# One greedy pass instead of tried orders: a change to the planner that writes out a kernel's instruction order

## The chip, the cores and the metric

The kernel runs on one core of one Trainium2 chip, as one program. The metric is the device time of that program in microseconds (us). Before the change the median of three runs is 1660.0 us (1659.27 to 1660.18). In the profile the engines are called PE (TensorE, the matrix products), PEld (its weight loads), DVE (VectorE), ACT (ScalarE), POOL (GpSimd) and SP (SyncE, which issues DMA transfers).

## The reference

All numbers are float32. An attention block without softmax feeds a mixture of four experts (8 batches, 8 heads, 576 tokens, 64 values a head; 4608 tokens of 512 values; experts of width 1024):

```python
kv  = np.einsum('bhsd,bhse->bhde', k, v)
o   = np.einsum('bhsd,bhde->bhse', q, kv)
x   = o / np.sqrt(np.mean(o * o, -1, keepdims=True) + 1e-06) * g_norm   # then to (4608, 512)
p   = domain_probs / (domain_probs.sum(-1, keepdims=True) + 1e-09)
for e in range(4):
    out += p[:, e:e+1] * (np.maximum(x @ w1[e], 0.0) @ w2[e])
```

## The kernel before, in words

**Steps.** The 4608 tokens are cut into nine chunks of 512: chunk c < 8 holds the first 512 tokens of batch c, and chunk 8 the 64 tokens that each batch has left over. The main loop runs over 4 experts x 9 chunks = 36 steps, numbered s = 0 to 35. A step has an up part (x @ w1 and the ReLU, `up`, line 1256; a plain form for step 0, `up_plain`, line 1360) and a down part (h @ w2, `down` at line 1488 or `down_deep` at line 1538), and the down part of step s is spread over the up part of step s + 1. While expert 0 is at work, `attention` (line 899) prepares the chunk after the present one; `opening` (line 760) prepares batch 0. A step past the opening takes some 43 to 53 us.

**Products by sevens.** Both parts use a Strassen-like scheme that makes a 2x2 block product of seven products, nested twice. So `up` has seven multipliers in the order `OUTER = (1, 2, 6, 5, 3, 7, 4)` and, for each, seven products in the order `ORDER = (1, 6, 2, 5, 7, 4, 3)`. One such product is 4 matmul calls; float32 takes two passes each, so the profile shows it as 8 matmuls of 128x128 on line 478 (`halves_of`). In the down part one unit is 8 or 16 of these, or 16 matmuls of 128x256. The forms that the products read (sums and differences of blocks) are made by `combine` (line 501) on DVE or POOL.

**Banks and copies.** A product's result lands in a PSUM bank. There are two each of four kinds: u1 and u2 for the up part, db and ab for the down part and for attention. For each multiplier, product 1 fills the bank u1, ACT copies it into the bank u2 as a seed (line 1305), product 2 adds onto the seed, and ACT copies that out as a block of the result (line 1305, out `big`). Products 6 and 7 are copied out as snapshots (line 1305, out `snap`), which DVE adds to products 5 and 3 (line 1313). The same pattern stands in `down_deep` at lines 1623 (ACT) and 1631 (DVE). Since a bank is filled again as soon as it has been read, most products wait for one ACT copy or one DVE sum that reads an earlier product. What stands between the two on PE is set by the order alone. Attention's rows are turned by PE into an ab bank (`turn_x`, line 1069) and copied by ACT in two halves (line 1081); the turn of the left-over rows is `turn_left` (line 1091); the key-value products are `key_values` (line 999); q, k and v come by loads on SP (line 507).

**What sets the order.** The scheduler of the framework is switched off (`manual_schedule`). Every piece of work is an `Op` with a key (its place in the sequence of steps, such as 19.06), a cost per engine that may run it, and its dependences. `Plan.layout` (line 94) plays the program through with these costs before the kernel is built, and writes down in which order each engine's operations start; the order list, and nothing else of it, becomes the program. At each moment each engine takes one operation that could start: PE and SP the first by key, the others the one that is due first. An operation may be taken up to 1.1 (PE) or 0.9 (DVE, ACT, POOL) of a step ahead of the first one pending. Combinations that DVE or POOL may make go to whichever is free. `begin` (line 310) books an operation; for an SP transfer it computes when it lands. In front of the first products PE is kept busy by transposes of the identity (line 1765).

`layout` does this step by step. For each step it saves its state, plays this step and the next one eight times (`TRIES, LOOK, SPREAD = 8, 1, 1`), the first time with the due times as they are and then with random shifts of 1 us, takes the draw with the least modelled idle time of PE, restores the state and plays the step for good:

```python
for step in sorted(steps):
    begin = self.save()
    ...
    for n in range(self.TRIES):
        ...
            op.due = op.base + (draw.gauss(0.0, self.SPREAD) if n else 0.0)
        if self.run(step + 1 + self.LOOK):
            tried.append((self.t - self.worked, n))
        self.restore(begin)
    n = min(tried)[1]
```

Of the kernel before, what the change touches and what calls it, by code (L numbers as in the profile page):

```python
# [41 lines left out]
class Plan:  # L42
# [18 lines left out]
    TRIES, LOOK, SPREAD = 8, 1, 1  # L61
# [32 lines left out]
    def layout(self, slots, later, idle, idle_banks, idle_until):  # L94

        self.idle = idle, idle_banks, idle_until
        self.free = {k: [(0.0, i) for i in range(len(v))] for k, v in slots.items()}
        self.slots = {k: list(v) for k, v in slots.items()}
        self.later = list(later)
        self.all_bufs = list(dict.fromkeys(b for op in self.ops for b in op.bufs))  # L100
        self.live = {}
        for b in self.all_bufs:
            self.live[b.kind] = self.live.get(b.kind, 0) + 1
        self.ended = {}
        self.todo = {e: [] for e in self.REACH}
        for n, op in enumerate(self.ops):
            op.n = n
            for e in op.cost:
                self.todo[e].append(op)
        for e in self.todo:  # L110
            self.todo[e].sort(key=lambda o: (o.key, o.n))
        keys, begun, spent = [], [], 0.0
        for op in self.todo["PE"]:
            keys.append(op.key)
            begun.append(spent)
            spent += op.cost["PE"]
# [4 lines left out]
        for op in reversed(self.ops):  # L121
            for d in op.deps:
                cross = self.SAME if op.cost.keys() == d.cost.keys() else self.CROSS
                d.due = min(d.due, op.due - cross - min(d.cost.values()))
        for op in self.ops:
            op.base = op.due
        self.missing, self.after = {}, {op: [] for op in self.ops}
        for op in self.ops:
            self.missing[op] = len(op.deps)
            for d in op.deps:  # L130
                self.after[d].append(op)
        self.waiting = {k: {} for k in self.SHARED}
        for op in self.ops:
            if not self.missing[op]:
                self.arm(op)
        self.first, known = {k: {} for k in self.INORDER}, set()
        for op in self.ops:
            for b in op.outs:
                if b.kind in self.first and b not in known:
                    known.add(b)  # L140
                    self.first[b.kind][op] = True
        self.busy = {e: 0.0 for e in self.todo}
        self.worked = 0.0
        self.bus, self.port = 3.8, 0.0
        self.lanes = [0.0] * self.LANES
        self.t = 0.0
        self.wake = [0.0, 1.6]
        self.left = len(self.ops)
        self.order = []

        steps = {}
        for op in self.ops:
            steps.setdefault(math.floor(op.key), []).append(op)
        for step in sorted(steps):
            begin = self.save()
            tried = []
            for n in range(self.TRIES):
                draw = random.Random(100 * n + step)
                for op in steps[step] + steps.get(step + 1, []):
                    op.due = op.base + (draw.gauss(0.0, self.SPREAD) if n else 0.0)  # L160
                if self.run(step + 1 + self.LOOK):
                    tried.append((self.t - self.worked, n))
                self.restore(begin)
            n = min(tried)[1]
            draw = random.Random(100 * n + step)
            for op in steps[step] + steps.get(step + 1, []):
                op.due = op.base + (draw.gauss(0.0, self.SPREAD) if n else 0.0)
            assert self.run(step + 1)
        self.run(math.inf)
        assert not self.left  # L170
        self.length = max(o.end for o in self.order)
        return self.order

    def save(self):
        copied = {
            name: {k: type(v)(v) for k, v in getattr(self, name).items()}
            for name in ("free", "slots", "todo", "waiting", "first")
        }
        copied.update({name: dict(getattr(self, name)) for name in ("live", "ended", "missing", "busy")})
        copied.update({name: list(getattr(self, name)) for name in ("later", "lanes", "wake", "order")})  # L180
        copied.update({name: getattr(self, name) for name in ("worked", "bus", "port", "t", "left")})
        return (
            copied, [(o.start, o.end, o.eng) for o in self.ops],
            [(b.left, b.slot, b.ap) for b in self.all_bufs],
        )

    def restore(self, saved):
        copied, ops, bufs = saved
        for name, value in copied.items():
            if isinstance(value, dict):  # L190
                value = {k: type(v)(v) if isinstance(v, (dict, list)) else v for k, v in value.items()}
            elif isinstance(value, list):
                value = list(value)
            setattr(self, name, value)
        for o, (o.start, o.end, o.eng) in zip(self.ops, ops):
            pass
        for b, (b.left, b.slot, b.ap) in zip(self.all_bufs, bufs):
            pass

    def arm(self, op):  # L200
        for b in op.outs:
            if b.kind in self.waiting and b.slot is None and "SP" not in op.cost:
                self.waiting[b.kind][op] = max([d.end for d in op.deps] or [0.0])

    def claimed(self, kind, op):
        return sum(
            1 for o, since in self.waiting[kind].items()
            if o.due < op.due and since <= self.t + self.AHEAD and o is not op
        )

    def ready(self, op, eng, front):
        when = 0.0
        for d in op.deps:
            if d.start is None:
                return None
        for d in op.deps:
            when = max(when, d.end + (self.SAME if d.eng == eng else self.CROSS))
        need = {}
        for b in op.outs:
            if b.kind is not None and b.slot is None:  # L220
                need[b.kind] = need.get(b.kind, 0) + 1
        for k, n in need.items():
            free = self.free[k]
            spare = self.SPARE.get(k, 0) if k != "xf" or op.key < self.FORMS else 0
            ahead = op.key > front + 0.1 and (eng == "SP" or op.early)
            if len(free) < n + (spare if ahead else 0):
                return None
            if k in self.waiting and len(free) < n + self.claimed(k, op):
                return None
            if k in self.first and any(o.due < op.due for o in self.first[k] if o is not op):  # L230
                return None
            when = max(when, sorted(free)[n - 1][0])
        if eng == "SP":
            when = max(when, self.lanes[0])
        if op.port:
            when = max(when, self.port)
        return when

    def run(self, until):

        wake, todo, busy = self.wake, self.todo, self.busy
        idle, idle_banks, idle_until = self.idle
        while self.left:
            t, moved = self.t, False
# [3 lines left out]
            if front >= until:  # L248
                return True
            for eng in todo:  # L250
# [10 lines left out]
                for op in pending:  # L261
# [8 lines left out]
                    when = self.ready(op, eng, front)  # L270
# [12 lines left out]
                if best is not None:  # L283
                    self.begin(best, eng)
                    moved = True
                if eng == "PE" and busy[eng] <= t and 1.6 <= t and front < idle_until:
                    kind, spare = next((
                        (k, f) for k in idle_banks for f in self.free[k] if f[0] <= t
                    ), (None, None))
                    if spare is not None:  # L290
# [3 lines left out]
                        op.fn = lambda eng, bank=self.slots[kind][spare[1]]: idle(bank)  # L294
                        busy[eng] = op.end
                        self.free[kind].remove(spare)
                        self.free[kind].append((op.end, spare[1]))
                        heapq.heappush(wake, op.end)
                        self.order.append(op)
# [5 lines left out]
            if not wake:  # L305
                return False
            self.t = heapq.heappop(wake)
        return True

    def begin(self, op, eng):  # L310
        t, wake, free = self.t, self.wake, self.free
        op.start, op.eng = t, eng
        if eng == "SP":
            self.busy[eng] = t + op.cost[eng]
            self.bus = max(self.bus, t + 1.5) + op.kb / 215.0
            op.end = self.bus + 0.5
            self.lanes = self.lanes[1:] + [op.end]
# [1498 lines left out]
```

## Time and profile before

| | |
|---|---|
| median of 3 runs | 1660.0 us |
| the profiled execution itself | 1660.0 us |
| its span, first to last instruction | 1657.7 us |
| PE busy | 1648.2 us (99%) |
| DVE, ACT, POOL busy | 1230.4, 978.0, 707.7 us (74, 59, 43%) |
| granted TensorE clock | 1.000 |
| DMA: mean rate | 140 GB/s, 220 to 235 GB/s in the first 124 us |

The profile is of one core. A row of a timeline gives the start in us, the length in us, engine, line, operation, out<-in, shape and count; in brackets stands the idle time before it and who ended it. PE works in a pipeline: a matmul of 128x128 is shown as 273 ns long, but the next one starts after some 55 ns, so the length of a PE row is the distance of its starts plus a tail of about 0.17 us. A wait of PE that is shorter than this tail shows no idle time at all; it is read from the distance of starts.

### The profile page before, as it was taken

The page shows a single profiled execution, that of the slowest core. Times are in us where ns is not written, and L with a number is a line of the kernel's source. Part 1 is how long each engine was busy: PE and PEld are TensorE (multiplying, and loading weights), DVE is VectorE, ACT ScalarE, POOL GpSimd, SP SyncE. Part 2 cuts the span into 40 slices and gives each one's busy share as a digit, 9 for nine tenths or more (in the row PEclk, how much of TensorE's full clock was granted, in tenths as well). Part 3 has the DMA queues.
Part 4 walks back from the last instruction along what each step waited for, and adds up shares of the span by engine and source line. Part 5 has one row for each costly group of instructions (what it writes and reads, how often), then busy time and mean ns, then how long its engine had stood idle before and what let it go on. Part 6 is the DMA issues. An engine that isn't in the chain of part 4 may idle for free.

```text
span 1657.7 us, 66538 instructions
## 1 busy us (share of the span) xinstructions
PE 1648.2 (99%) x28990; PEld 1557.9 (94%) x28990; DVE 1230.4 (74%) x2150; ACT 978.0 (59%) x2421; POOL 707.7 (43%) x671
## 2 busy tenths in 40 slices
PE   8999999999999999999999999999999999999998
PEld 6688888888899999999999999999999999999996
DVE  4677768776877778777778787777778787777774
ACT  3465555554456665666556666666666566666662
POOL 4542232223244454553345554433455545443341
PEclk9999999999999999999999999999999999999999
DMA  9985665624475353544558444444577544444442
GB/s 221 208 235 140 195 174 157 164 100 164 146 202 139 96 136 112 133 118 120 149 150 193 115 117 122 108 110 113 141 185 176 120 124 117 117 106 114 116 104 52
DMA packets 202860, 232.44 MB, mean 140 GB/s; under 512 B 92936, under 2 KB 142536, under 8 KB 202568
## 3 DMA queue, kind: packets, MB, share of 16 engines
q1 hardware_dynamic: 179016, 191.41, 38.9%
q0 software_dynamic: 23552, 36.78, 14.4%
q8 instruction: 227, 3.72, 0.9%
q14 instruction: 65, 0.53, 0.1%
HBM read 153.95 MB, written 74.19 MB: 138 GB/s over the span
## 4 chain that ended last, share of the span: by engine, by line
PE 99%; issue 0%; ACT 0%; POOL 0%; DVE 0%; POOLq 0%
PE u L478 48%; PE db L478 32%; PE ab L478 15%; PE ab L1004 1%; PE ab L1031 1%; PE ab L1072 1%; PE ab L1765 0%; PE ab L789 0%; PE ab L809 0%; PE db L1040 0%; PE db L829 0%; PE ab L1093 0%; PE ab L844 0%; PE db L864 0%; ACT big L1453 0%
## 5 line engine op out<-in xcount | busy, mean ns | idle before, releaser
L501 DVE TENSOR_TENSOR big<-big,big 128x256 f32<-128x256 f32 (+1 forms) x568 | 517.4, 931 | 23.7 <-ACT big L1269 11.8
L478 PE MATMUL u<-xf,big 128*64 128x128 f32 x7072 | 513.3, 273 | 0.0
L478 PEld LDWEIGHTS u<-xf,big 128*64 128x64 f32 x7072 | 412.6, 137 | 5.6 <-issue 0.7
L478 PE MATMUL u<-xf,w1y 128*64 128x128 f32 x5304 | 392.4, 273 | 0.0
L478 PE MATMUL db<-big,big 128*64 128x128 f32 (+1 forms) x4208 | 352.5, 308 | 0.1
L1313 DVE TENSOR_TENSOR big<-u,snap 128x256 f32<-128x256 f32 x468 | 196.9, 422 | 202.8 <-PE u L478 154.1
L478 PEld LDWEIGHTS u<-xf,w1y 128*64 128x64 f32 x5304 | 310.4, 137 | 2.8 <-issue 0.8
L1305 ACT ACTIVATE snap<-u 128x256 f32<-128x256 f32 x490 | 187.6, 383 | 185.1 <-PE u L478 163.5
L478 PEld LDWEIGHTS db<-big,big 128*64 128x64 f32 x4208 | 257.0, 137 | 40.9 <-issue 0.8
L501 POOL TENSOR_TENSOR big<-big,big 128x256 f32<-128x256 f32 (+1 forms) x151 | 212.1, 1409 | 177.3 <-DVE big L501 94.6
L1305 ACT ACTIVATE big<-u 128x256 f32<-128x256 f32 x468 | 178.3, 383 | 68.6 <-PE u L478 43.1
L501 POOL TENSOR_TENSOR big<-big 128x512 f32<-128x512 f32 (+1 forms) x95 | 116.4, 1226 | 145.6 <-DVE big L501 88.0
L1623 ACT ACTIVATE snap<-db 128x256 f32<-128x256 f32 (+1 forms) x230 | 82.3, 358 | 137.0 <-PE db L478 123.2
L1269 ACT ACTIVATE big<-big 128x1024 f32<-128x1024 f32 x136 | 142.9, 1051 | 4.5 <-DVE big L501 3.4
L1631 DVE TENSOR_TENSOR big<-ab,snap 128x256 f32<-128x256 f32 x170 | 71.6, 421 | 69.6 <-ACT snap L1623 37.2
L1476 POOL DMA_DIRECT2D out_dram<-big x120 | 104.3, 1097 | 42.7 <-ACT big L1453 35.9
L1305 ACT ACTIVATE u<-u 128x256 f32<-128x256 f32 x245 | 90.9, 372 | 35.4 <-PE u L478 24.0
L1661 POOL TENSOR_TENSOR big<-big 128x512 f32<-128x512 f32 x27 | 34.4, 1274 | 150.7 <-DVE big L501 129.5
L478 PE MATMUL db<-w2y,big 128*64 128x128 f32 x1328 | 97.7, 273 | 0.0
L1453 ACT ACTIVATE big<-big,p_all 128x256 f32<-128x256 f32 x198 | 93.7, 500 | 1.4 <-POOL big L1661 0.7
L478 PE MATMUL db<-small,big 128*64 128x128 f32 x1248 | 93.2, 273 | 0.5 <-ACT snap L1623 0.5
L501 DVE TENSOR_TENSOR big<-big 128x512 f32<-128x512 f32 (+1 forms) x114 | 91.4, 806 | 0.5 <-PE db L478 0.4
(188 smaller groups left out, 2314.3 us busy)
## 6 DMA issues: line engine op xcount, KB each, us to landing
xf<-x SPq DMA_DIRECT2D x104, 512.0 KB, 3.8
xf<-x_h SPq DMA_DIRECT2D x85, 256.0 KB, 3.4
out_dram<-big POOLq DMA_DIRECT2D x80, 256.0 KB, 6.3
xf<-x SPq DMA_DIRECT2D x78, 256.0 KB, 3.7
x<-xf SPq DMA_DIRECT2D x36, 512.0 KB, 3.9
big<-in_moe_w_dram SPq DMA_DIRECT2D x29, 512.0 KB, 5.9
x_h<-big SPq DMA_DIRECT2D x18, 512.0 KB, 3.3
big<-in_moe_w_dram POOLq DMA_DIRECT2D x18, 512.0 KB, 7.2
```

The costliest lines, as they stand in the source:

```text
L478: nc.tensor.matmul(out_[cols], lhsT=lhsT[:, cols], rhs=rhs, **kw)
L501: lambda eng: adder(eng).tensor_tensor(out=out_(), in0=a(), in1=b(), op=op),
L1004: nc.tensor.matmul(bank.ap[r * D:(r + 1) * D, o * D:(o + 1) * D], lhsT=ks[r], rhs=vs[r], start=(j == 0), stop=(j == len(sets) - 1), skip_g ...
L1031: nc.tensor.matmul(raw[r].ap[c * D:(c + 1) * D, (o * NR + t) * D:(o * NR + t + 1) * D], lhsT=qt.ap[half, col:col + D], rhs=kv.ap[half, o * ...
L1269: lambda eng: nc.scalar.activation(out=b.ap[:], in_=b.ap[:], func=ACT.Relu),
L1305: lambda eng: nc.scalar.activation(out=where(), in_=ps.ap[:, 0:HN], func=ACT.Copy),
L1313: lambda eng: nc.vector.tensor_tensor(out=block(whole, a, t), in0=src.ap[:, 0:HN], in1=add_.ap[:], op=ALU.add),
L1453: lambda eng: nc.scalar.activation(out=cell(i, half), in_=ap(), func=ACT.Copy, scale=prob()),
L1476: nc.gpsimd.dma_start(out=dst, in_=cell(i)[parts, :], accum_op=ALU.add)
L1623: lambda eng: nc.scalar.activation(out=where(), in_=group_of(ps.ap), func=ACT.Copy),
L1631: lambda eng: nc.vector.tensor_tensor(out=cell(tq, dq), in0=group_of(src.ap), in1=group_of(add_.ap), op=ALU.add,),
L1661: lambda eng: adder(eng).tensor_tensor(out=whole(to), in0=whole(a), in1=whole(b), op=ALU.add),
```

## The change

The words that go with the change tell of batch 0 from contiguous loads with tokens at 9p+j, products pair of heads by pair, probabilities fetched early by GpSimd, and chunk 0's forms in expert 1. All these stand in both kernels. The diff touches `Plan` alone:

- The tries go, and with them `save` and `restore`. There is one pass, with the due times unshifted. `run`, `ready`, `arm`, `claimed` and `begin` are folded into `layout`.
- The model of an SP transfer differs. Before, it joins the bus 1.5 us after its issue and lands 0.5 us after its turn; after the change these are 0.6 and 1.9 us. The bus is free at first from 3.8 us before, and from 2.6 us after.
- The kernel proper, its operations, their keys, costs and dependences are the same, so that only the order on each engine and the choice between DVE and POOL (or ACT and DVE) can differ.

```diff
-    TRIES, LOOK, SPREAD = 8, 1, 1
...
-        self.bus, self.port = 3.8, 0.0
+        bus, port = 2.6, 0.0
...
-        for step in sorted(steps):
-            begin = self.save()
-            tried = []
-            for n in range(self.TRIES):
-                draw = random.Random(100 * n + step)
-                for op in steps[step] + steps.get(step + 1, []):
-                    op.due = op.base + (draw.gauss(0.0, self.SPREAD) if n else 0.0)
-                if self.run(step + 1 + self.LOOK):
-                    tried.append((self.t - self.worked, n))
-                self.restore(begin)
-            n = min(tried)[1]
-            draw = random.Random(100 * n + step)
-            for op in steps[step] + steps.get(step + 1, []):
-                op.due = op.base + (draw.gauss(0.0, self.SPREAD) if n else 0.0)
-            assert self.run(step + 1)
-        self.run(math.inf)
...
+        while left:
+            moved = False
             while todo["PE"] and todo["PE"][0].start is not None:
                 todo["PE"].pop(0)
             front = todo["PE"][0].key if todo["PE"] else 1e9
-            if front >= until:
-                return True
...
-            self.bus = max(self.bus, t + 1.5) + op.kb / 215.0
-            op.end = self.bus + 0.5
+                        bus = max(bus, t + 0.6) + op.kb / 215.0
+                        op.end = bus + 1.9
```

In the built programs the change shows as follows. Every operation of one is in the other. PE has 46 transposes of the identity in place of 44, the two more in front of the first key-value product. Past them the order on PE is the same up to 63 us, on SP up to 64 us, on ACT up to 42 us, on DVE and POOL up to 45 us of the profile before. In step 16 and in steps 32 to 36 (36 is the last down part) PE, ACT, DVE and POOL have the same order in both, and SP has it in most steps from 11 on. DVE has 4 instructions fewer, ACT 6 fewer and POOL 10 more. In step 1 SP loads the last quarter of v of batch 2 (`v2_3`, two transfers) 17 transfers later than before.

## The prediction

> **What bounds the kernel now.** I read the page's parts 1 and 4 first (does one engine set the end?), then PE's waits, the windows, and timelines at PE's few waits. From the page, and the list of PE's waits over the whole span (engine and line, for whom, us in total, times, longest):
>
> ```profile
> span 1657.7 us, 66538 instructions
> PE 1648.2 (99%) x28990; PEld 1557.9 (94%) x28990; DVE 1230.4 (74%) x2150; ACT 978.0 (59%) x2421; POOL 707.7 (43%) x671
> PE 99%; issue 0%; ACT 0%; POOL 0%; DVE 0%; POOLq 0%
> ```
>
> ```profile
> PE ab L789 <- issue: 1.6, 1, 1.6
> PE db L829 <- issue: 1.5, 1, 1.5
> PE ab L1765 <- POOL ident masks.py:199: 1.4, 1, 1.4
> PE db L478 <- ACT snap L1623: 0.5, 1, 0.5
> ```
>
> PE is the chain from start to end and hardly ever stands: 1657.7 - 1648.2 = 9.5 us, of which 1.4 lie before its first instruction, 1.5 and 1.6 are two pauses in the opening (at 13 and 19 us), 0.5 is a wait at 1627 us, and 4.4 the tail after its last matmul. In between it is full (window, length, busy us of PE, PEld, DVE, ACT, POOL, clock, DMA share, GB/s):
>
> ```profile
> 41.40:1616.00 1574.60, 1574.41 (x27968) 1504.90 (x27966) 1191.91 (x2075) 952.12 (x2361) 680.04 (x639) 1.00 0.54 140
> ```
>
> So a new order has almost nothing to win: it takes no work from PE, and outside the start and the tail there are some 4 us of waits. It can lose whatever waits it puts in.
>
> **The price of a product placed too near.** A changed order harms PE where a product follows too closely the one whose copy it needs. First the pace, undisturbed (start, length):
>
> ```profile
> 1441.25 0.61 PE L478 MATMUL ab<-small,big 128*64 128x128 f32 x8
> 1441.68 0.61 PE L478 MATMUL ab<-kv,big 128*64 128x128 f32 x8
> 1442.12 0.61 PE L478 MATMUL u<-xf,w1y 128*64 128x128 f32 x8
> ```
>
> A product starts every 0.437 us and shows 0.61. The trace of before has a few products too near. At 88 us, PE and ACT:
>
> ```profile
> 88.29 1.75 PE L478 MATMUL u<-xf,big 128*64 128x128 f32 x24
> ...
> 88.94 0.38 ACT L1305 ACTIVATE snap<-u 128x256 f32<-128x256 f32 x1
> 89.38 0.42 PEld L478 LDWEIGHTS u<-xf,big 128*64 128x64 f32 x8 [0.29 <-ACT snap L1305]
> ```
>
> The product that starts at 88.29 ends at 88.90; ACT starts its snapshot 0.04 later and takes 0.38; the product that waited for it starts at 89.38. From start to start that is 1.09 us. The waiting product stands second behind the first, where 2 x 0.437 = 0.874 was its turn: **0.22 us** lost. Directly behind, it would lose 1.09 - 0.437 = **0.65**; third behind (1.31) nothing. The second price is seen too, at the end:
>
> ```profile
> 1626.39 1.04 PE L478 MATMUL db<-w2y,big 128*64 128x128 f32 x16
> 1627.90 0.66 PE L478 MATMUL db<-small,big 128*64 128x128 f32 x8 [0.47 <-ACT snap L1623]
> ```
>
> Two products take 1.51 us to the next start in place of 0.874: the third needs the copy of the second, and 0.64 is lost.
>
> **The change, part by part.** The work on PE is the same but for two transposes. DVE has 4 instructions fewer, ACT 6 fewer, POOL 10 more; DVE is 74% busy, so a moved combination costs only where PE wants it next. So the change is worth what its order puts in as waits, less those it removes. I went through the new order and counted, for every product that needs an ACT copy or a DVE sum of an earlier product, how far behind it stands. Counted in the old order, the same way gives five waits in all: 0.34, 0.22 and 0.22 in step 1 (the last vanishes behind the second), 0.55 and 0.12 in the last down part. The trace shows 0.31 (a product at 67.97, the next at 68.71, less 0.437), 0.22, 0.64 and 0.13. The count finds every wait and is right to 0.1 us. In the new order it finds:
>
> - *Step 1, around 63 to 67 us.* Product 2 of multiplier 1 directly behind product 1: 0.65. Then `turn_left` (line 1091) directly behind the second `turn_x` (line 1069), whose first half-copy on ACT (line 1081, 0.68) must free its bank: the turn shows 1.19 and PE's next turn comes after 1.02, so 1.19 + 0.05 + 0.68 + 0.06 - 1.02 = 0.96. Then product 1 of multiplier 2 needs the second half-copy, 0.63 later, behind a `turn_left` of 0.37: 0.26. Sum 1.87.
> - *Steps 4 and 6.* Product 4 of multiplier 2 second behind product 7: 0.22, and on ACT a 0.6 us evacuation of attention starts just ahead of the snapshot and holds it 0.12 longer: 0.34 each, 0.68.
> - *Step 7.* Product 1 of multiplier 3 second behind the product whose copy frees its bank, 0.22; a down unit waits for its bank until ACT and DVE have merged the one before (0.50 + 0.48, lines 1453 and 1460, behind two snapshots), 0.35. Sum 0.57.
> - *Steps 9 to 13, 24, 27.* Four places within 0.03 to 0.14 of their turn, 0.44 if all come; I take half, 0.22.
> - *Step 19.* Product 5 of multiplier 1 directly behind product 2 of multiplier 2, whose copy frees its bank: 0.65. A product 4 second behind a product 7: 0.22. A seed of `down_deep` stands in ACT's order behind a 1.05 us negation of a weight block: 0.31. Sum 1.18.
> - *Step 28.* The same neighbours as in step 19: 0.65. Product 3 directly behind product 5, whose DVE sum (0.42, line 1313) must have read the bank, 1.13 - 0.437 = 0.70. One more second-behind: 0.22. Sum 1.57.
>
> In steps 32 to 36 the orders are equal and the end's waits stay. The other steps have none. Sum 1.87 + 0.68 + 0.57 + 0.22 + 1.18 + 1.57 = 6.1; gone with the old order of step 1: 0.31 + 0.22 = 0.5. **Net +5.6.**
>
> *The opening.* Two more transposes of the identity before the first key-value product, at the pace there (8 in 1.09 us with the tail): 0.13 each. They are hidden if the 1.49 us pause that follows covers them. Between 0 and +0.27; I take 0.1, as the pause is the nearest row.
>
> *v of batch 2.* Two transfers (`v2_3`) are moved behind 17 others on SP (16 of q, one store). Eight of q take 4.32 us to issue (65.96), so 17 come 9.2 us later. Its reader `key_values` has 2.1 us to spare now (landed at 69.36, read at 71.45) and itself moves back 6.1 us in PE's order, by the products now ahead of it: 2.1 - 9.2 + 6.1 = -1.0. The 1.87 of waits ahead of it in the same step cover that, as long as SP isn't held by them: eight of the q loads wait for the second `turn_x`, which stands behind only 0.65 of those waits. So its cost is between nothing and, at SP's slowest gaps and the longest landing of such loads there (6.8 against its own 4.7), some 1.0 + 2.1 = 3. I take 0, since its own row says 4.7. The other loads of SP and the accumulating weight load of step 19 (9.6 us on POOL's queue; such loads have a median of 7.2) move by one or two places and land with at most 0.1 to catch up; from -0.3 to +0.9.
>
> *The clock.* The pauses of 1.49 and 1.63 us stand in windows with a granted clock of 1.00; all waits above are single and shorter than 1.0. So a wait costs its own length and no more. The Trainium skill ("TensorE: Matmul & The Clock Gate", section "HAM oscillation — how this bites in real kernels") speaks against filling PE's order with waits, as pauses of over 3.4 us make the clock fall to half. By that rule only a wait for `v2_3` near its upper end, joined to the others, could come near; it would then add some 1.7 us (an estimate from that page). No row of before shows it.
>
> The profiled execution took 1660.0 us, which is also the median of the runs, 2.3 more than its span. 1660.0 + 5.6 + 0.1 = **1665.7 us**.
>
> **The rivals.**
>
> 1. *The waits stand, and `v2_3` comes late.* For: the DMA engines are over 90% busy up to 83 us, and PE's margin is negative without the other waits. Against: its own landing row. It would add 1 to 3: 1667 to 1669, with landings worse than any there 1671.
> 2. *Not slower by anything to be measured: the opening's pauses go.* One mechanism, at 13 and 19 us: PE stands 1.5 and 1.6 us for nothing that the profile names ("issue"). They come after its 222nd and its 349th matmul. If the two added transposes shift them to where PE would wait for a copy anyway, 3.1 us are given back: 5.7 - 3.1 = 2.6, 1662.6 us, inside 0.2%. It decides from 2.4 us given back on. Against: both pauses would have to go, and two matmuls are a small shift.
> 3. *The order does less than the count says.* Places where I have ACT or DVE held by other work (0.24 in steps 4 and 6, 0.35, 0.22, 0.31, 0.70: together 1.8) come out free, because these engines run ahead more than their order shows: 5.7 - 1.8 = 3.9, 1663.9. With half the 0.65s read too high as well it ends under 1663.3. For: ACT is only 59% busy. Against: the count on the old order erred by less than 0.1 a place.
>
> **How the numbers follow.** About 0.2% (3.3 us) is what a measurement of this kernel can tell from no change. Chances: the forecast with its small errors (1663.3 to 1668), 0.68; rival 1 beyond that, 0.14; rival 2, 0.08, of which 0.01 faster; rival 3 under 1663.3, 0.09; anything that makes it faster besides, 0.01. So slower 0.82, same 0.16, faster 0.02. The range goes from rival 2's 1662.3 to rival 1's upper end, 1670.5: what lies outside is some 0.06 below and 0.07 above, and a little for what I haven't thought of.
>
> **What would show it.** In the profile after, PE's waits should appear on ACT lines 1241, 1017 and DVE line 1249 (the old 1305, 1081 and 1313), at some 63 to 70, 230, 335, 395, 905 and 1290 us, none over 1.1; PE's busy time only about 2 us up, since waits under the 0.17 tail are shown as busy in part; the two pauses near 13 and 19 us; the wait of 0.5 near the end. `v2_3` should land within 0.3 us of its reader's turn. It is wrong if PE waits for a DMA over 1 us, if a long wait stands in a step that I call free (8, 14 to 18, 20 to 23), or if the clock falls below 1.00.

## The result, and the profile after

After the change the median is 1665.62 us (1665.14 to 1665.92), beside 1659.63 us (1658.87 to 1660.18) before: a ratio of 1.0036 with a 95% interval of 1.0019 to 1.0053, so 6.0 us slower. Two single executions of the experiments below fell far out of all others (4969 us of `newdma_turn`, 9892 us of `v_early_turn`) and are left out of the ratios. The profiled execution took 1665.3 us with a span of 1663.6. Lines of the code after are those of before less 64: the products are on line 414, ACT's copies on 1241 and 1559, DVE's sums on 1249 and 1567, `combine` on 437.

The page after, its parts 1 and 4:

```profile
span 1663.6 us, 66539 instructions
PE 1650.9 (99%) x28992; PEld 1558.8 (94%) x28992; DVE 1252.9 (75%) x2146; ACT 980.6 (59%) x2415; POOL 694.4 (42%) x681
PE 97%; DVE 1%; issue 1%; ACT 0%; POOL 0%; DMA 0%; SPq 0%; DVEq 0%; POOLq 0%; ACTq 0%
```

The list of PE's waits of the kernel after (for whom, us in total, times, longest):

```profile
PE ab L725 <- issue: 1.7, 1, 1.7
PE db L765 <- issue: 1.5, 1, 1.5
PE u L414 <- DVE big L1249: 0.8, 2, 0.6
PE db L414 <- ACT snap L1559: 0.7, 2, 0.5
PE u L414 <- ACT small L1241: 0.5, 1, 0.5
PE u L414 <- ACT big L1241: 0.5, 1, 0.5
PE u L414 <- ACT u L1241: 0.5, 1, 0.5
PE ab L1029 <- ACT big L1017: 0.3, 1, 0.3
```

And its windows, over the same stretch as before:

```profile
41.40:1616.00 1574.60, 1571.27 (x27862) 1499.90 (x27860) 1210.47 (x2064) 951.18 (x2347) 666.88 (x649) 1.00 0.54 140
```

The two pauses of the opening stand as they were, the clock is 1.00, and PE is still the chain. New are seven waits of 0.2 to 0.6 us for ACT's copies and DVE's sums. The idle time in this window is 3.3 us, 3.1 more than before; the other half of the loss lies under the tails of PE's rows, as told of the profile before, and is read from the distance of starts. Counted so, against each shape's undisturbed pace, PE's last product starts 5.90 us later than before, and this divides as follows:

| stretch of the span | predicted | measured | what is in it |
|---|---|---|---|
| opening, to 60 us | +0.1 | +0.09 | two transposes |
| 60 to 100 us (step 1) | +1.34 | +0.64 | 0.64, 0.41, 0.07, 0.40 new; 0.31, 0.22 gone |
| 100 to 500 us (steps 4, 6, 7) | +1.25 | +1.19 | 0.31, 0.31, 0.22 |
| 500 to 1400 us (steps 9 to 28) | +2.97 | +3.97 | 0.16, 0.13; 0.71, 0.22, 0.13; 0.08, 0.38; 0.73, 0.82, 0.22 |
| end | 0 | 0.01 | 0.64 and 0.13 in both |

The last column is the time by which single products start late. What it lacks to the measured column are many differences of 0.05 to 0.15 where PE goes from one kind of work to another, and 0.05 behind each wait (shown below). The dearest place is step 28, on PE (start, length, idle time before it and who ended it):

```profile
1291.57 0.64 PE L414 MATMUL u<-xf,w1y 128*64 128x128 f32 x8
1292.01 0.64 PE L414 MATMUL u<-xf,big 128*64 128x128 f32 x8
1293.17 0.66 PE L414 MATMUL u<-xf,w1y 128*64 128x128 f32 x8 [0.53 <-ACT big L1241]
1294.43 1.09 PE L414 MATMUL u<-xf,w1y 128*64 128x128 f32 x16 [0.60 <-DVE big L1249]
```

From 1292.01 to 1293.17 are 1.16 us in place of 0.44: a product directly behind the one whose copy it needs. From 1293.17 to 1294.43 are 1.26: directly behind one whose DVE sum must first have read the bank.

### The profile page after: what moved, and what is told of

The parts are those of the page before. It is cut to its first block, busy times and chain, and to the rows that moved or that the text cites. A ratio compares the mean times of both kernels' runs of the same rounds, so it can differ in the third digit from the quotient of the medians.

```text
span 1663.6 us, 66539 instructions
## 1 busy us (share of the span) xinstructions
PE 1650.9 (99%) x28992; PEld 1558.8 (94%) x28992; DVE 1252.9 (75%) x2146; ACT 980.6 (59%) x2415; POOL 694.4 (42%) x681
## 4 chain that ended last, share of the span: by engine, by line
PE 97%; DVE 1%; issue 1%; ACT 0%; POOL 0%; DMA 0%; SPq 0%; DVEq 0%; POOLq 0%; ACTq 0%
PE u L414 47%; PE db L414 32%; PE ab L414 14%; PE ab L967 1%; PE ab L940 1%; PE ab L1008 1%; DVE big L437 0%; PE ab L1701 0%; PE ab L725 0%; PE ab L745 0%; DVE big L1597 0%; PE db L976 0%; PE ab L1029 0%; DMA small<-in_q_dram 0%; PE db L765 0%
## 5 line engine op out<-in xcount | busy, mean ns | idle before, releaser
L437 DVE TENSOR_TENSOR big<-big,big 128x1024 f32<-128x1024 f32 (+1 forms) x592 | 549.5, 950 | 26.6 <-ACT big L1205 8.6
L414 PE MATMUL u<-xf,big 128*64 128x128 f32 x6496 | 474.5, 273 | 0.1
L414 PEld LDWEIGHTS u<-xf,big 128*64 128x64 f32 x6496 | 381.3, 137 | 4.7 <-issue 0.7
L414 PE MATMUL db<-big,big 128*64 128x128 f32 (+1 forms) x4368 | 368.3, 307 | 0.7 <-ACT snap L1559 0.7
L414 PEld LDWEIGHTS db<-big,big 128*64 128x64 f32 x4368 | 269.0, 137 | 39.9 <-issue 2.1
L437 POOL TENSOR_TENSOR big<-big,big 128x256 f32<-128x256 f32 (+1 forms) x157 | 206.0, 1316 | 196.5 <-DVE big L437 101.2
L1559 ACT ACTIVATE snap<-db 128x256 f32<-128x256 f32 (+1 forms) x230 | 82.2, 358 | 121.5 <-PE db L414 109.2
L414 PE MATMUL db<-small,big 128*64 128x128 f32 (+1 forms) x1528 | 116.7, 274 | 0.0
L437 DVE TENSOR_TENSOR big<-big 128x512 f32<-128x512 f32 (+1 forms) x121 | 102.1, 853 | 0.0
L414 PE MATMUL ab<-big,big 128*64 128x128 f32 (+1 forms) x1384 | 97.5, 276 | 0.0
L414 PEld LDWEIGHTS db<-small,big 128*64 128x64 f32 x1528 | 90.8, 137 | 0.9 <-issue 0.2
```

What stands on the lines that cost most here:

```text
L414: nc.tensor.matmul(out_[cols], lhsT=lhsT[:, cols], rhs=rhs, **kw)
L437: lambda eng: adder(eng).tensor_tensor(out=out_(), in0=a(), in1=b(), op=op),
L1559: lambda eng: nc.scalar.activation(out=where(), in_=group_of(ps.ap), func=ACT.Copy),
```

## The experiments

**Theories.** A: the one pass places products too near the copies that they need, and the tries of before were what took these places out; each costs its distance. B: the changed landing model of SP's transfers does it, since other loads come late. C: the old order is a tuned whole, and any other order costs some time. For step 1, D came up on the way: DVE works in order and stands at a transposition of q whose load has not landed, with a sum behind it that PE needs.

### One half of the change at a time

`tries_newdma` is the kernel before with the new landing model alone:

```diff
-        self.bus, self.port = 3.8, 0.0
+        self.bus, self.port = 2.6, 0.0
...
-            self.bus = max(self.bus, t + 1.5) + op.kb / 215.0
-            op.end = self.bus + 0.5
+            self.bus = max(self.bus, t + 0.6) + op.kb / 215.0
+            op.end = self.bus + 1.9
```

> The kernel before with only the landing model of SP transfers exchanged; the tries stay. Theory A (PE waits at products placed too near behind the one whose copy they need, and the tries take such places out): the count on this order finds 2.3 us of waits against 1.5 in the kernel before, so +0.8, 1660.4 us. Theory B (the other landing model, that is, the order of the loads, makes the difference): as after, 1665.6. Theory C (any other order costs, because DVE and POOL share the work otherwise and their queues run differently): the orders of all steps up to 30 differ from before, 1662 to 1666.

Measured: 1661.69 us beside 1660.05, ratio 1.0010 (1.0001 to 1.0019). It is 1.6 us, more than A expected and far from the whole. Its trace has no wait behind 350 us but the two of the end. That alone says little, as the orders differ less than was expected: in the order lists, PE, DVE, ACT and POOL differ from before only in steps 0 to 14, 21 and 22. Most of the loss is one wait in step 1, PE and DVE of `tries_newdma`:

```profile
79.97 0.61 PE L478 MATMUL u<-xf,big 128*64 128x128 f32 x8
80.48 1.38 DVE L978 STREAM_TRANSPOSE small<-small 128x1152 f32<-128x1152 f32 x1 [1.96 <-DMA small<-in_q_dram]
81.78 0.39 DVE L1313 TENSOR_TENSOR big<-u,snap 128x256 f32<-128x256 f32 x1
82.22 0.66 PE L478 MATMUL u<-xf,w1y 128*64 128x128 f32 x8 [1.65 <-DVE big L1313]
```

DVE is idle for 1.96 us until the last load of q2_1 has landed, then transposes for 1.38; the sum that frees a bank for PE stands behind both, and PE's product starts 1.82 us late. This is where D comes from.

`onepass_olddma` is the kernel after with the old landing model (the same three lines the other way).

> The kernel after with the old landing model; no tries. Theory A: the count finds 8.8 us of waits, 7.3 more than in the kernel before and 1.6 more than in the one after, of which some 0.8 in step 1 are counted too high (the two turns and their copies): 1666 to 1667 us. Theory B: as before, 1659.6. Theory C: 1662 to 1668, no place named.

Measured: 1666.26 us beside 1660.05, ratio 1.0039 (1.0026 to 1.0051), as A expected. The waits are of the same kinds in partly other places, and one of 0.48 us in `key_values` at 78.6 us is for a load of v; the list of PE's waits shows a part of it:

```profile
PE ab L940 <- DMA kv<-in_v_dram: 0.3, 1, 0.3
```

So the loss comes when the tries go, with either landing model, and B falls as the main cause.

### The tries in some steps only

Both are `tries_newdma` with one line changed, which gives the tries to a part of the steps. `tries_late` has them where the two costliest places of the kernel after are:

```diff
-            for n in range(self.TRIES):
+            for n in range(self.TRIES if step in (18, 19, 27, 28) else 1):
```

> The kernel after (one pass, new landing model), but with the eight tries in steps 18, 19, 27 and 28 alone. Theory A: the waits that the trace of after shows in steps 19, 24 and 28 go (0.71 + 0.22 + 0.13 + 0.08 + 0.38 + 0.73 + 0.82 + 0.22 = 3.3), all others stay: 1662.3 us, and the trace has the same waits as after up to 890 us and none from there to 1625. Theory B: no load has to do with it, 1665.6. Theory C: 1664 to 1667.

Measured: 1662.89 us beside 1660.05, ratio 1.0019 (1.0010 to 1.0028). The waits of steps 19, 24 and 28 are gone, those before step 18 are there with the same lengths (0.64, 0.41, 0.31, 0.31, 0.22, 0.16, 0.13), but for step 1's 0.40, which is 0.15 here, and 0.07, which is gone. One of 0.12 is new at 1036 us.

`tries_early` has them in the steps under 18 (`if step < 18 else 1`).

> The opposite part: the eight tries in all steps below 18, one pass from 18 on. Theory A: the waits of steps 19, 24 and 28 stay (3.3), those of steps 4, 7, 9 and 11 go, and step 1 has other, smaller ones; the count falls by 1.9 from that of after: 1663.7 us. Together with the run with late tries alone the two savings should add up to what all tries save. Theory B: 1665.6 or, if the load of v alone matters, whatever step 1 makes of it. Theory C: no sum is expected.

Measured: 1666.18 us beside 1660.05, ratio 1.0036 (1.0022 to 1.0050), which misses by 2.5. As expected, the waits of steps 4, 7, 9 and 11 are gone and those of 19, 24 and 28 stand. But step 1 has a new wait of 1.34 us at 82.2, of the same kind as in `tries_newdma`. Such a wait stands in four of the orders laid out with the new landing model (1.82 in `tries_newdma`, 1.34 here, 0.40 in the kernel after, 0.15 in `tries_late`) and in neither of the two with the old one. DVE stands at this load in the old orders as well (2.23 us in before, 1.54 in `onepass_olddma`), but there nothing that PE wants at once is behind it. That the new model's landing times put the transposition too early is the likely reason, but it is argued from this. 1.34 of the miss is this wait; others of 0.33 and 0.17 in step 1 and 0.23 in step 3 make most of the rest.

### The price by itself, with its control

`near40` is the order of before, in which forty products go one place back on PE, so that the product that needs their copy stands second behind them and no longer third. They lie in steps 10 to 29.

```diff
     order = plan.layout(slots, later, idle, ("ab", "db"), 0.0)
...
+    for n, count in (...):
+        at = next(i for i, o in enumerate(order) if ... o.n == n)
+        to = at
+        while count:
+            to += 1
+            count -= order[to].eng == "PE"
+        order.insert(to, order.pop(at))
```

> The kernel before with 40 products in steps 10 to 33 each moved behind the next product on PE, so that the product that follows stands second instead of third behind the one whose copy it needs. Nothing else is changed. Theory A: each place loses 0.22 us, 40 x 0.22 = 8.8: 1668.4 us, and 40 waits of 0.22 stand in the trace. Theory B (loads): nothing, 1659.6. Theory C (a changed order as such costs): as much as the run with 40 other swaps.

Measured: 1670.42 us beside 1659.58, ratio 1.0065 (1.0052 to 1.0078): +10.8, that is 0.27 a place and not 0.22. The trace of `near40` shows where the 0.05 is, on PE:

```profile
730.64 0.61 PE L478 MATMUL u<-xf,big 128*64 128x128 f32 x8
731.08 0.61 PE L478 MATMUL db<-w2y,big 128*64 128x128 f32 x8
731.73 0.66 PE L478 MATMUL u<-xf,big 128*64 128x128 f32 x8
732.22 0.61 PE L478 MATMUL ab<-big,big 128*64 128x128 f32 x8
732.66 0.61 PE L478 MATMUL db<-w2y,big 128*64 128x128 f32 x8
```

The starts lie 0.44, 0.65, 0.49 and 0.44 apart. The waiting product loses 0.22 (0.15 to 0.31 over the forty), and the one behind it 0.05 again: the row that waited is 0.66 long instead of 0.61. Over the forty places the trace sums to 8.85 + 1.98 = 10.83. Its list of PE's waits shows none of them; besides the start and the two pauses of the opening it has one line, the wait near the end that before has too:

```profile
PE db L478 <- ACT snap L1623: 0.5, 1, 0.5
```

PE's busy time is 8.4 us up instead (1656.6), and its busy share is 99% as before. A reader of these two would not find the waits.

`swap40` is the control: forty other products (steps 10 to 28) are moved one place in the same way, where nothing stands too near afterwards.

> The control: also 40 products of steps 10 to 33 moved behind the next one on PE, but at places where the count finds that nothing comes nearer than third behind. Theory A: no wait, 1659.6 us. Theory C: the same loss as in the run with 40 near places.

Measured: 1659.74 us beside 1659.58, ratio 1.0000 (0.9991 to 1.0008). So C falls for PE: another order on PE as such costs nothing that these times can tell. The orders of DVE, ACT, POOL and SP are untouched here, so this run does not speak of them; `newdma_turn` below does.

### Mending the order by hand

`repair` is the kernel after, in which eight products go back by one to three places on PE, in steps 4, 6, 7, 19 and 28 and in the last down part (the same loop as in `near40`, other numbers).

> The kernel after with eight products of steps 4, 6, 7, 19, 28 and 36 moved back by one to three places on PE, to put more work between a product and the copy that it needs; DVE, ACT, POOL and SP keep their order. Theory A: the count falls from 7.2 to 5.2 us, of which 0.4 in step 36, where both kernels wait: 1663.6 us. Theory B and C: 1665.6 or more.

Measured: 1663.44 us beside 1659.58, ratio 1.0025 (1.0016 to 1.0034). The waits of 0.31, 0.31 and 0.22 are gone, 0.71 and 0.73 have become 0.28 and 0.30, and the end's 0.64 and 0.13 have become 0.20. That is 2.2 us less than the kernel after, by eight moves.

`before_rep` does the same to the kernel before: three products, one in step 1 and two in the last down part, one place each.

> The kernel before with three products moved by one place on PE, one in step 1 and two in step 36. Theory A: the count falls from 1.5 to 0.6 us: 1658.7 us, which the times can hardly tell from the kernel before; the trace should show the wait of 0.31 at 68 us gone and those of 0.64 and 0.13 at 1627 us down to some 0.14. If the end waits for something other than that copy, they stay.

Measured: 1658.64 us beside 1659.58, ratio 0.9995 (0.9987 to 1.0004). The 0.31 is gone and the end's 0.77 has become 0.20. New are 0.17 at 68.4 us, where `turn_left` now stands behind that product and waits for DVE, and 0.24 at 90 us. Its span of 1656.9 us is the shortest of the profiled ones, but 0.5 of that is a shorter pause in the opening, and the interval of the times does not tell it from before.

### The load of v, and DVE's queue

`v_early` is the kernel after with the two `v2_3` loads put back ahead of the second set of q loads.

```diff
+    late = [o for o in order if o.eng == "SP" and o.outs[0].name == "v2_3"]
+    order = [o for o in order if o not in late]
+    to = next(i for i, o in enumerate(order) if o.eng == "SP" and o.outs[0].name == "q2_1")
+    order[to:to] = late
```

> The kernel after with the two loads of the last quarter of v of batch 2 put back in front of the second set of q loads on SP (8 q loads and one store earlier). Theory A: these loads land just at their reader's turn in after and cost nothing, so 1665.6 us. Rival (the load comes late and holds PE): the wait of 0.40 at 80 us goes, and up to 1 us more.

Measured: 1666.87 us beside 1659.59, ratio 1.0044 (1.0029 to 1.0059). It got no faster: the load of v was not late in the kernel after. But the q loads now are, and DVE of `v_early` waits for them longer:

```profile
79.48 1.38 DVE L914 STREAM_TRANSPOSE small<-small 128x1152 f32<-128x1152 f32 x1 [2.61 <-DMA small<-in_q_dram]
80.78 1.18 DVE L437 TENSOR_TENSOR big<-big,big 128x1024 f32<-128x1024 f32 x1
81.88 0.41 DVE L1249 TENSOR_TENSOR big<-u,snap 128x256 f32<-128x256 f32 x1
```

PE's wait behind this sum grew from 0.40 us in the kernel after to 1.45.

`v_later` puts the `v2_3` loads four transfers further back than the kernel after has them.

> The kernel after with the same two loads put four SP transfers later still. Theory A, with the load's margin used up in after: four transfers at 0.5 us each make the key-value products wait some 2 us, 1667.6 us, one wait of PE for a DMA at 78 us, and perhaps a store or two more that hold SP. If there was slack left: 1665.6.

Measured: 1671.57 us beside 1659.59, ratio 1.0078 (1.0061 to 1.0094): +6.0 against the kernel after, where +2.0 was expected. PE of `v_later`, at `key_values` (line 940) and behind it:

```profile
77.80 0.75 PE L940 MATMUL ab<-kv 120*64 120x64 f32 x20
82.34 0.80 PE L940 MATMUL ab<-kv 120*64 120x64 f32 x20 [3.79 <-DMA kv<-in_v_dram]
82.97 0.77 PE L414 MATMUL u<-small,big 128*64 128x128 f32 x8
83.52 1.07 PE L414 MATMUL u<-xf,w1y 128*64 128x128 f32 x8
84.38 1.07 PE L414 MATMUL u<-big,w1y 128*64 128x128 f32 x8
```

The windows there (the third number from the right is the granted clock):

```profile
80.00:82.00 2.00, 0.00 (x0) 0.00 (x0) 1.02 (x3) 0.00 (x0) 0.93 (x2) 1.00 1.01 288
84.00:86.00 2.00, 2.00 (x22) 2.00 (x20) 0.51 (x2) 0.55 (x2) 0.00 (x0) 0.50 1.06 279
88.00:90.00 2.00, 2.00 (x28) 1.57 (x26) 1.81 (x6) 0.77 (x2) 0.10 (x1) 1.00 0.07 23
```

Two things were under-estimated. The loads came 3.6 us later and not 2 (landed at 82.48 in place of 78.85), so PE lost 4.0. And behind an idle time of 3.79 us the clock fell to 0.50: products start 0.86 apart, twice 0.43, until about 86.7 us, for another 1.7. Less the 0.40 and 0.07 that such a wait covers and 0.3 in which the opening's pauses were shorter, that makes 4.9; PE's last product starts 4.8 later. The remaining 0.9 of the span lies behind PE's last product, and I can't place it.

D itself was tried by a move on DVE alone: the transposition of q2_1 goes five DVE instructions back. `newdma_turn` does this to `tries_newdma`, `v_early_turn` to `v_early`:

```diff
+    to = at = next(i for i, o in enumerate(order) if o.eng == "DVE" and o.outs[0].name == "q2_1")
+    count = 5
+    while count:
+        to += 1
+        count -= order[to].eng == "DVE"
+    order.insert(to, order.pop(at))
```

> The kernel with tries and the new landing model, with one DVE instruction moved: the transposition of the second set of q of batch 2 (line 978) stands five DVE instructions later. Theory D (the wait of 1.82 us at 80 us in that kernel is DVE's: its queue stands at this transposition until the last q load has landed, and the sum that PE needs next stands behind it): the 1.82 goes and nothing else changes, 1661.7 - 1.8 = 1659.9 us. Rival (PE waits at 80 us for the key-value products' load itself, whatever DVE does): 1661.7.

> The kernel after with v of batch 2 loaded earlier (1666.9 us, with a wait of 1.45 us at 80 us), and with the same transposition five DVE instructions later. Theory D: the sum on line 1249 that PE waits for no longer stands behind it, and the wait of 1.45 goes: 1665.4 us. The rival: 1666.9.

Measured: `newdma_turn` 1660.20 us beside 1659.79, ratio 1.0002 (0.9993 to 1.0011); `v_early_turn` 1665.18, ratio 1.0030 (1.0020 to 1.0041). Both as D expected: 1.82 and 1.45 us of wait are gone. PE and DVE of `newdma_turn`, at the place shown above for `tries_newdma`:

```profile
80.44 0.42 DVE L1313 TENSOR_TENSOR big<-u,snap 128x256 f32<-128x256 f32 x1 [1.45 <-PE u L478]
80.66 0.61 PE L478 MATMUL u<-xf,big 128*64 128x128 f32 x8
81.10 0.61 PE L478 MATMUL u<-xf,w1y 128*64 128x128 f32 x8
```

The sum now comes as soon as PE has delivered, and the products keep their 0.44. With the landing model's one wait moved, the new model is level with the old. This also answers the rest of C: on PE, DVE, ACT and POOL its orders differ from before in steps 0 to 14, 21 and 22, and that costs nothing beyond the wait.

## Why the prediction was right, and where its terms were not

**The mechanism held.** 1665.7 us was predicted (+5.7), 1665.6 measured (+6.0). Theory A stands by four kinds of runs: without the tries alone the kernel loses as much (`onepass_olddma`), with them in four steps the places there vanish (`tries_late`), forty such places made by hand cost what they should but for 0.05 (`near40`, `swap40`), and moving single products back gives the time back (`repair`). All new waits of PE but those at 73.8 and 79.8 us stand in places that were counted, none is over 1.1 us, and the steps called free (8, 14 to 18, 20 to 23) have none. (The stated range of 1662.3 to 1670.5 is not quite what its rivals give, 1662.6 and 1671; nothing rests on that.)

**That the sum came out so near is partly luck.** Two terms were off, by 0.7 and 1.0 us, in opposite directions.

- *Step 1: 1.34 predicted, 0.64 measured.* Product 2 behind product 1 cost 0.64, as counted. `turn_left` cost 0.41 and not 0.96, and the 0.26 behind it nothing. Here is the step that failed: the copy was taken to start when the whole turn is done ("1.19 + 0.05 + 0.68"; the rows of the turn show 1.09, not 1.19). PE and ACT of the kernel after:

```profile
68.00 1.09 PE L1008 MATMUL ab<-ident,small 128*128 128x128 f32 x8
68.69 1.26 ACT L1017 ACTIVATE big<-ab,gcol 128x512 f32<-128x512 f32 x2
69.44 0.44 PE L1029 MATMUL ab<-ident,snap 128*128 128x128 f32 x2 [0.34 <-ACT big L1017]
```

  The copy starts 0.69 behind the turn's start, when four of its eight transposes are done: each half-copy needs four of them and not all. It looked otherwise in the trace of before, at the first turn of the same step (PE and ACT):

```profile
65.17 1.09 PE L1072 MATMUL ab<-ident,small 128*128 128x128 f32 x8
66.30 1.26 ACT L1081 ACTIVATE big<-ab,gcol 128x512 f32<-128x512 f32 x2 [0.54 <-PE ab L1072]
```

  There the first copy starts 1.13 behind the turn's start, but in the old order list ACT takes the second half of this turn first; in the new list it takes the first half first. Against this stands a wait that I had not counted, 0.40 at 79.8 us. DVE and PE of the kernel after:

```profile
77.79 1.38 DVE L914 STREAM_TRANSPOSE small<-small 128x1152 f32<-128x1152 f32 x1 [1.66 <-DMA small<-in_q_dram]
79.09 1.18 DVE L437 TENSOR_TENSOR big<-big,big 128x1024 f32<-128x1024 f32 x1
80.20 0.41 DVE L1249 TENSOR_TENSOR big<-u,snap 128x256 f32<-128x256 f32 x1
80.67 0.66 PE L414 MATMUL u<-big,w1y 128*64 128x128 f32 x8 [0.23 <-DVE big L1249]
```

  It is theory D, and its load is one of q. I had watched the load of v, whose reader is PE, and let DVE's own loads pass with "at most 0.1 to catch up".
- *Steps 4, 6, 7: 1.25 predicted, 1.19 measured.* The three places came at 0.31, 0.31 and 0.22; the 0.35 for the down unit's bank did not come. Three times 0.05 behind the waits and other small differences, which were not counted, make up for most of it.
- *Steps 9 to 28: 2.97 predicted, 3.97 measured.* The places are the counted ones. Missing were 0.05 behind each wait (0.4 in all; the prediction had "a wait costs its own length and no more"), 0.2 at step 28's two products, and 0.3 at step 24, where I halved four small places to 0.22. There the snapshot stands in ACT's order behind a scaling of 0.91 that itself waited for POOL, as ACT and PE of the kernel after show:

```profile
1206.93 0.91 ACT L1389 ACTIVATE big<-big,p_all 128x256 f32<-128x256 f32 x2 [1.18 <-POOL big L1597]
1207.74 0.25 ACT L1559 ACTIVATE snap<-db 128x128 f32<-128x128 f32 x1
1208.14 0.66 PE L414 MATMUL db<-big,big 128*64 128x128 f32 x8 [0.21 <-ACT snap L1559]
```

  The seed in step 19 that was to cost 0.31 cost 0.13.
- *`v2_3`: 0 predicted, 0 measured.* `key_values` runs undisturbed. Rival 1 was wrong for the kernel after, but near: PE waits 0.48 for such a load in `onepass_olddma`, and `v_later` shows that four transfers more make it 6 us, above the 3 that I had as its upper end. There the last of the two loads is issued 2.85 us later and takes 3.45 us to land in place of 2.67, and the clock joins in.
- *Rival 2* didn't come: the pauses are 1.5 and 1.7 us. They stand behind PE's 222nd and 349th matmul as before, though two transposes more are ahead of them, so they go by PE's count and not by the place in the program. *Rival 3* is refuted: 0.70 came as 0.82, 0.24 in steps 4 and 6 as 0.2, and only 0.35 and a part of 0.31 came free.

## What to carry to other kernels

Where one in-order engine is full from start to end, a new order is priced by walking through it and asking of each instruction how far behind its producer's copy it stands; the gain of a search over orders is the sum of the places that it avoids, and forty places cost forty times one. Walk the other engines' queues as well: a load needs no reader on the full engine to stop it, since what stands behind the load's reader on DVE is late too. And read the distance of starts, not the idle or busy time, where the waits are shorter than the tail of a modelled row.

## What the runs showed of the hardware

- **The product behind a wait is late as well.** In `near40` forty products that waited 0.22 us in the mean are each followed by a start 0.05 late, and the same shows behind the kernel after's waits.
- **The clock falls after pauses of under 2 us in the opening.** The Trainium skill ("TensorE: Matmul & The Clock Gate", section "HAM oscillation — how this bites in real kernels") puts the limit at idle gaps of about 3.4 us. `v_later` agrees: 3.79 us idle, then 0.50, and 1.7 us lost, as the prediction had estimated from that page. But in the profiled execution of `tries_early` one of the opening's pauses was a little longer than usual (1.95 us, where the kernel after has 1.69), and there the clock fell too. PE, and then the windows, of `tries_early`:

```profile
22.06 0.50 PE L789 MATMUL ab<-ident,big 64*64 64x64 f32 x10 [1.95 <-issue]
```

```profile
22.00:24.00 2.00, 1.94 (x49) 1.61 (x48) 0.11 (x1) 1.19 (x3) 0.00 (x0) 0.72 0.76 102
24.00:26.00 2.00, 2.00 (x37) 1.88 (x38) 0.58 (x1) 0.69 (x1) 0.00 (x0) 0.50 0.23 34
```

  PE's products there lost 1.5 us. In `v_early` a pause of 1.80 us at 13.9 us was followed by a clock of 0.52 in the same way; PE lost some 1.5 us against the kernel after, which the second pause, gone in this execution, gave back. In the other profiled executions the opening stayed at 1.00, with pauses of up to 1.7 us, and of 1.80 in `swap40`. So in this opening, among small matmuls of 64x64, the clock can fall behind a pause of some 1.8 us and need not; what decides it is not shown. The measurement decides here, and the prediction's remark that only a wait of over 3.4 us could touch the clock was too easy.
- **The opening's pauses come with transfers of instructions.** In all 14 profiled executions they stand behind PE's 222nd and 349th matmul (the second is missing in `v_early`), 256 instructions of PE and its weight loads apart. In the DMA records each of the 27 ends 1.3 to 1.9 us after a transfer of 16384 bytes on the queue named "instruction" has ended. In `before` such transfers end at 13.27 and 19.72 us, and PE goes on at 14.92 and 21.25; in `tries_early` the second ends at 20.26, and PE goes on at 22.06. So PE most likely waits there for its next block of instructions, and the pause is longer when that block comes later or PE gets there sooner. No run tests this.
